# A fused attention and mixing kernel: another order of its one list of steps, with the DMA transposes of batch 3 at other places

## The chip, the cores and the metric

The kernel runs on one core of a Trainium2 chip. The metric is device time in microseconds (us) of one execution; the number given for a version is the median of its runs. The times of a profile are those of one profiled execution, counted from the first instruction of the program.

The core has five engines that each work through an instruction list of their own, in order: TensorE (PE, matmuls; its weight loads are listed as PEld), VectorE (DVE), ScalarE (ACT), GpSimd (POOL) and SyncE (SP). SP does no arithmetic here; it issues DMAs. An engine that waits for a semaphore holds back all that stands behind it in its list. Matmuls write to PSUM, which has eight banks.

## The reference

Four batches of 768 tokens. An attention with 8 heads of 64 and a local window, and then a token and channel mixing of its output:

```python
scores = scale * np.matmul(q, k.transpose(0, 1, 3, 2))
scores = scores + bias[None, :, :, :]          # -slope(head) * distance
scores = np.where(keep, scores, -1000000000.0) # 96 nearest earlier keys and the first 8
...
a = a / (np.sum(a, axis=-1, keepdims=True) + 1e-09)
return np.matmul(a, v).astype(np.float32)
```

```python
theta = x @ w_theta
cos_t, sin_t = (np.cos(theta), np.sin(theta))
zr = x * cos_t
zi = x * sin_t
yr = np.einsum('ts,bsd->btd', w_tok_r, zr)
yi = np.einsum('ts,bsd->btd', w_tok_i, zi)
y = yr + yi
u = x + y
return (u + np.maximum(u @ w_ch, 0.0)).astype(np.float32)
```

Here x is the attention's output with its heads side by side (768 x 512 per batch).

## The kernel before

The whole work is cut into 660 steps. A list of words, `order`, holds them in one sequence; a loop at the end reads a word such as `pd.3.2.1` and calls the step `pd` with the arguments 3, 2, 1. Scheduling is by hand for all five engines: each engine gets its instructions in the order in which the list names them, and only semaphores (for data, for a reused buffer, for a reused PSUM bank) hold an engine back. A second list of digits says which PSUM bank each step takes. So the list sets the order on each engine, and not the time: a step of SP that stands behind a step of GpSimd in the list does not wait for it.

The first argument of a step is the batch (0 to 3), for most. In the attention the second is a pair of heads (0 to 3); T is 128, so a batch has six token tiles.

- Loads, issued by GpSimd: `lq` (q and k of some heads), `lv` (v), `lw`, `lt`, `lc` (the three weights). Batch 3 is loaded by `lq.3.0.4` (heads 0 to 3) and `lq.3.4.4` (heads 4 to 7), each as eight DMAs of one head, and `lv.3.0.8`. Between the first and the second stands `gt.1.2`, a copy of one element on GpSimd which waits until `z.1.1.0` has written its part; so the second half and v of batch 3 are issued only then.
- qT and kT (64 x 2 heads on partitions): for batches 0 to 2, `pc` copies a pair of q (last argument 0) or k (1) together on DVE, `q` transposes it on PE, and `qe` copies the result out of PSUM. For batch 3, `pd` is one DMA transpose issued by SP (L312), 128 x 768 in two bytes, so 192 KB. `kg` (L322, L323) copies keys shifted by a tile next to the 8 global keys (kG), on DVE or ACT; it needs kT.
- `s` (L362): scores of two token tiles; `e` (L374): exponential on ACT; `x` (L383, L386): times a table of biases on DVE, which `bt` has made. `vg` (L397, L398) prepares v as `kg` does k; `v` (L421): weights times v; `n` (L432, L434): division by the sum, into x_sb.
- xT: `xd` (L443) is a DMA transpose of a pair of heads of x_sb, issued by SP; for some pairs `xt` on PE and `xe` do it. `th` (L477): theta, in parts (`th.b.c.0` and `.6` use the pairs 0 to 2 of xT, `.3` the pair 3); `sn` (L487, L489): sine and cosine on ACT (`sin` loads their table ahead); `z` (L498): zr and zi on DVE.
- `w` and `we`: transposes of the two token weights and their copies out. `m` (L511): four matmuls of the token mixing of one token tile; `u` (L519): x + y on DVE.
- uT: `ud` (L529) is a DMA transpose of a tile of u (128 KB) issued by SP, or `ut` on PE with the copy `ue` (L539). `c` (L550): four matmuls with w_ch, which need uT; `r` (L558): the sum with the relu on DVE; `st` (L564): the store of 256 KB, issued by SP, the last half by ACT.

A letter at the end of a copy step (`.a`, `.v`) says on which of ACT and DVE it is made. qT, kT and kG have six buffers each, u six, uT five, o four, x_sb two, xT one.

SP's list in the stretch in question, before:

```
xd.1.0 st.0.1 xd.1.1 st.0.0 pd.3.1.0 st.0.2 ud.1.0 ud.1.1 pd.3.0.0 pd.3.2.1 ud.1.2 pd.3.1.1 st.0.3
xd.2.0 st.0.5 xd.2.2 xd.2.1 pd.3.0.1 st.0.4 pd.3.3.1 st.1.0 ud.1.4 ud.1.5 ud.1.3 pd.3.2.0 st.1.1 pd.3.3.0
```

Of the kernel before, what the change touches and what calls it, by code (L numbers as in the profile page):

```python
# [16 lines left out]
def kernel(  # L17
# [105 lines left out]
    dist = const.tile([T, 6, T], BF)  # L123
# [20 lines left out]
    diag = const.tile([T, H, T], BF)  # L144
# [422 lines left out]
    def do(op, *a):  # L567
        ops[op](*a)
# [1 line left out]


    order = """
        warm.1.3 diag.2 warm.6.0 dist diag.0 bt.6 diag.1 sb.0.1 cast.1.1.a cast.0.0.v warm.3.1 bt.0
        cast.0.1.a diag.3 cast.1.0.v bt.4 q.0.1.0 q.0.0.0 qe.0.1.0.v.2 q.0.0.1 qe.0.0.0.a.0
        qe.0.0.1.a.0 qe.0.0.0.a.1 q.0.1.1 kg.0.0.0.1.v qe.0.0.1.v.1 lw.0 sb.0.0 qe.0.1.1.a.2 swap
        s.0.0.0 kg.0.0.1.4.a sb.0.2 kg.0.1.0.4.v q.0.2.0 lt.0.2 e.0.0.0 q.0.2.1 qe.0.2.0.v.2 lt.2.4
        s.0.0.1 s.0.0.2 e.0.0.1 sb.1.0 qe.0.2.1.v.2 s.0.1.0 warm.1.2 e.0.1.0 sb.1.1 kg.0.2.0.4.v
        sb.1.2 vg.0.0.4 e.0.0.2 s.0.1.1 lw.2 s.0.1.2 sb.2.0 e.0.1.2 v.0.0.0.0.6 v.0.0.1.0.6 e.0.1.1
        s.0.2.0 n.0.0.1.0.6 lq.1.0.8 q.0.3.0 e.0.2.0 q.0.3.1 n.0.0.0.0.6 sb.2.1 qe.0.3.1.a.2
        qe.0.3.0.v.2 s.0.2.1 v.0.1.0.0.6 e.0.2.1 xt.0.0.0.6 sb.3.1 xe.0.0.0.6.v sb.3.0 kg.0.3.0.4.v  # L580
        sb.2.2 mv.1 s.0.2.2 s.0.3.1 n.0.1.0.0.6 e.0.2.2 s.0.3.0 v.0.1.1.0.6 vg.0.4.4 e.0.3.0 sb.3.2
# [68 lines left out]
_INS = ['q', 'k', 'v', 'n_global', 'n_local', 'moe_w_theta', 'moe_w_tok_r', 'moe_w_tok_i', 'moe_w_ch']  # L650
_OUTS = [((4, 768, 512), 'float32')]
# [30 lines left out]
```

## Time and profile before

| what | value |
|---|---|
| median of 3 runs | 169.82 us (169.81 to 170.51) |
| the profiled execution | 170.19 us |
| its span, first to last instruction | 168.1 us |
| granted TensorE clock | 1.00 |
| busy: PE / DVE / ACT / POOL | 154.2 / 124.8 / 106.6 / 38.5 us |
| instructions | 3796 |

How to read the lines: in a group, `x24 | 16.2, 684 | 11.2 <-PE bank L511 11.0` means 24 instructions that were busy for 16.2 us in total, of 684 ns each, and 11.2 us in which the engine stood idle just before them, 11.0 of them ended by a PE instruction of line 511. A timeline line starts with the time of its first instruction and the time that the group took; in brackets stands the idle time before it and what ended it. A line of the chain has start, duration and what it was; "DMA kT<-qk" there is the time from the issue of that transpose to its landing. SP's and POOL's DMA lines give the time of the issue, not of the transfer. PE's matmuls overlap each other, so a group's busy time is not a sum of durations.

### The profile page before, as it was taken

What the parts mean: (1) busy time and instruction counts of PE and PEld (TensorE: products, weight loads), DVE (VectorE), ACT (ScalarE), POOL (GpSimd) and SP (SyncE); (2) the same over time, 40 slices, a digit from 0 to 9 for tenths busy, and PEclk for the clock granted to TensorE, in tenths of its full rate; (3) what the DMA queues carried; (4) which work ended last, traced back from release to release, by engine and by line L of the source; (5) the groups of instructions that cost most, each with busy time, mean ns of one, the idle gap of its engine ahead of it and who ended that gap; (6) DMA issues with size and microseconds to landing.
All of it is one profiled execution on the core that took longest, in us unless ns stands there. A gap on an engine that the chain in (4) does not pass through costs nothing.

```text
span 168.1 us, 3796 instructions
## 1 busy us (share of the span) xinstructions
PE 154.2 (92%) x1547; PEld 86.2 (51%) x1569; DVE 124.8 (74%) x257; ACT 106.6 (63%) x142; POOL 38.5 (23%) x46
## 2 busy tenths in 40 slices
PE   7899999999999996999987798899999999999990
PEld 2456685555657573545553543345557444444450
DVE  7697986978999998695994991588789438543571
ACT  3899899898789937898866115988871349100010
POOL 8975348050352102079400000000000000000000
PEclk9999999999999999999999999999999999999999
DMA  5999999999999999989999998560125674344456
GB/s 150 199 171 177 209 209 203 204 208 188 149 199 193 148 191 149 78 137 121 154 118 146 205 108 207 113 156 4 31 47 158 127 172 174 100 44 125 125 206 231
DMA packets 72704, 25.34 MB, mean 151 GB/s; under 512 B 60784, under 2 KB 69744, under 8 KB 72688
## 3 DMA queue, kind: packets, MB, share of 16 engines
q0 software_dynamic: 45696, 12.45, 82.0%
q1 hardware_dynamic: 26576, 12.13, 34.8%
q10 hardware_dynamic: 416, 0.52, 0.9%
q8 instruction: 12, 0.20, 0.5%
q14 instruction: 4, 0.03, 0.1%
HBM read 25.69 MB, written 6.29 MB: 190 GB/s over the span
## 4 chain that ended last, share of the span: by engine, by line
PE 59%; DMA 18%; DVE 15%; issue 2%; SPq 2%; ACT 1%; POOL 0%; DVEq 0%; POOLq 0%
PE bank L511 27%; PE bank L477 9%; PE bank L550 9%; DMA kT<-qk 8%; DMA xT<-x_sb 6%; PE bank L362 4%; PE bank L421 4%; DMA qk<-in_q_dram 3%; DVE e L383 2%; DVE x_sb L434 2%; DVE kT L299 2%; PE bank L265 2%; SPq L312 1%; DMA uT<-u 1%; DVE kG L322 1%
## 5 line engine op out<-in xcount | busy, mean ns | idle before, releaser
L511 PE MATMUL bank<-zri,w_tokT 128*128 128x512 bf16 x273 | 66.8, 379 | 1.4 <-issue 1.0
L374 ACT ACTIVATE e<-bank 128x1024 bf16<-128x1024 f32 (+1 forms) x48 | 42.9, 955 | 8.9 <-PE bank L362 8.3
L511 PEld LDWEIGHTS <-w_tokT 128*128 128x128 bf16 x288 | 26.5, 98 | 29.5 <-DVE w_tokT L269 0.2
L550 PE MATMUL bank<-w_ch_bf,uT 128*128 128x512 bf16 (+1 forms) x98 | 24.1, 370 | 2.4 <-DVE u L519 1.6
L477 PE MATMUL bank<-w_theta_bf,xT 128*128 128x512 bf16 x92 | 22.8, 379 | 2.9 <-DMA xT<-x_sb 2.7
L519 DVE TENSOR_TENSOR u<-x_sb,bank 128x512 bf16<-128x512 bf16 x24 | 16.2, 684 | 11.2 <-PE bank L511 11.0
L558 DVE SCALAR_TENSOR_TENSOR o<-bank,u 128x512 f32<-128x512 f32 (+1 forms) x25 | 16.2, 666 | 7.9 <-PE bank L550 7.5
L498 DVE TENSOR_TENSOR zri<-x_sb,cs 128x1024 bf16<-128x1024 bf16 (+1 forms) x30 | 16.6, 580 | 6.1 <-ACT cs L489 4.0
L434 DVE TENSOR_TENSOR x_sb<-bank,rec 128x768 bf16<-128x768 f32 (+2 forms) x21 | 16.1, 767 | 0.7
L550 PEld LDWEIGHTS <-uT 128*128 128x128 bf16 x100 | 9.3, 98 | 12.3 <-issue 1.8
L477 PEld LDWEIGHTS <-xT 128*128 128x128 bf16 x96 | 8.8, 97 | 13.0 <-DMA xT<-x_sb 3.9
L539 ACT COPY uT<-bank 128x512 bf16<-128x512 bf16 x5 | 2.9, 589 | 19.1 <-PE bank L535 19.1
L383 DVE TENSOR_TENSOR e<-e,etab 128x1024 bf16<-128x1024 bf16 (+1 forms) x24 | 14.1, 618 | 0.9 <-ACT e L374 0.9
L421 PEld LDWEIGHTS <-e 128*128 128x128 bf16 x352 | 12.6, 97 | 3.3 <-issue 1.0
L362 PE MATMUL bank<-qT,kT 64*128 64x128 bf16 x224 | 12.9, 218 | 0.4 <-DVE qT L299 0.3
L421 PE MATMUL bank<-vn,e 128*128 128x65 bf16 x224 | 13.2, 193 | 0.1
L489 ACT ACTIVATE cs<-bank,halfpi 128x1024 bf16<-128x1024 f32 x8 | 8.9, 1116 | 6.2 <-PE bank L477 6.2
L362 PEld LDWEIGHTS <-kT 64*128 64x128 bf16 x224 | 8.6, 94 | 6.3 <-issue 5.4
L92 POOL DMA_DIRECT2D vn<-in_v_dram x5 | 9.6, 1922 | 8.1 <-DVE qkn L306 6.9
L362 PE MATMUL bank<-qT,kG 64*128 64x128 bf16 x128 | 10.7, 216 | 0.0
L421 PE MATMUL bank<-vG,e 128*128 128x65 bf16 x128 | 10.4, 193 | 0.1
L86 POOL DMA_DIRECT2D qk<-in_q_dram x8 | 6.9, 864 | 12.4 <-issue 4.7
(76 smaller groups left out, 199.1 us busy)
## 6 DMA issues: line engine op xcount, KB each, us to landing
out_dram<-o SPq DMA_DIRECT2D x23, 256.0 KB, 2.4
vn<-in_v_dram POOLq DMA_DIRECT2D x3, 768.0 KB, 23.1
qk<-in_q_dram POOLq DMA_DIRECT2D x2, 768.0 KB, 20.3
qk<-in_k_dram POOLq DMA_DIRECT2D x2, 768.0 KB, 22.3
w_nat<-in_moe_w_tok_r_dram POOLq DMA_DIRECT2D x3, 384.0 KB, 12.3
w_nat<-in_moe_w_tok_i_dram POOLq DMA_DIRECT2D x3, 384.0 KB, 13.5
vn<-in_v_dram POOLq DMA_DIRECT2D x2, 384.0 KB, 9.8
qk<-in_q_dram POOLq DMA_DIRECT2D x8, 96.0 KB, 9.5
```

Of the source, the lines that this page charges most:

```text
L92: nc.gpsimd.dma_start(out=vn[:, h0:h0 + n, :, 0:D].rearrange("p h t d -> p (h t) d"), in_=v[b, h0:h0 + n].rearrange("h (t p) d -> p (h t) ...
L362: nc.tensor.matmul(pb[:, hh, o:o + T], lhsT=lhsT, rhs=qT[R, (own, nxt)[part]], start=bool(b), stop=bool(b) or (jt == NT - 1 or (j == 1 and ...
L374: nc.scalar.activation(e_c, ps_of["s", b, p, c][:, :, 0:blocks(c) * T], AF.Exp, scale=scale)
L383: nc.vector.tensor_mul(e_c, e_c, tab[:, :, s0:s0 + n].rearrange("p a s n -> p a (s n)"))
L421: nc.tensor.matmul(po4[:, head - h0, it - i0], lhsT=l_, rhs=r_, start=(i_ == 0), stop=(i_ == len(mms) - 1))
L434: nc.vector.tensor_mul(xv, po4[:, :, :, 0:D], rec.to_broadcast([T, m_, nt, D]))
L477: nc.tensor.matmul(ps_of["th", b, c][j_], lhsT=xT_sb[b][:, dc, (2 * c + j_) * T:(2 * c + j_ + 1) * T], rhs=w_theta_bf[:, dc, :], start=(dc ...
L498: nc.vector.tensor_mul(zri[b][:, i_, tt, :].rearrange("p j (g d) -> p j g d", g=NP), x_sb[b][:, :, tt, :].rearrange("p g j d -> p j g d"), ...
L511: nc.tensor.matmul(ps_of["m", b, tt], lhsT=w_tokT[wi][:, st, tt * T:(tt + 1) * T], rhs=zri[b][:, wi, st, :], start=(mixed[b, tt] == 0), st ...
L519: nc.vector.tensor_add(u_sb[b, tt].rearrange("p (g d) -> p g d", g=NP), x_sb[b][:, :, tt, :], ps_of["m", b, tt].rearrange("p (g d) -> p g ...
L550: nc.tensor.matmul(ps, lhsT=uTs[b, tt][:, dc, :], rhs=w_ch_bf[:, dc, own], start=(dc == 0), stop=(dc == NC - 1))
L558: nc.vector.scalar_tensor_tensor(o_sbs[b, tt][:, own], in0=ps_of["c", b, tt, part], scalar=0.0, in1=u_sb[b, tt][:, own], op0=ALU.max, op1= ...
```

## The change

The list is replaced by another order of the same steps, and the bank digits with it. No step is added or left out; 34 copy steps change between ACT and DVE, 17 in each direction. GpSimd's sequence of steps stays as it is. SP's list in the same stretch is now:

```
xd.1.0 xd.1.1 st.0.0 st.0.1 pd.3.0.1 pd.3.1.1 ud.1.0 st.0.5 xd.2.0 st.0.4 ud.1.3 pd.3.3.1 xd.2.1
xd.2.2 st.0.2 pd.3.0.0 ud.1.2 st.0.3 ud.1.5 ud.1.1 pd.3.1.0 pd.3.2.1 st.1.3 pd.3.3.0 pd.3.2.0 ud.1.4
```

In the common list `lv.3.0.8` stands behind `pd.3.1.0`, `ud.1.0` and `ud.1.1` before, and behind `pd.3.0.1`, `pd.3.1.1` and `ud.1.0` now. The diff, cut to the rows of interest (the last rows of both parts are the end of the list):

```diff
...
-        s.0.0.1 s.0.0.2 e.0.0.1 sb.1.0 qe.0.2.1.v.2 s.0.1.0 warm.1.2 e.0.1.0 sb.1.1 kg.0.2.0.4.v
-        sb.1.2 vg.0.0.4 e.0.0.2 s.0.1.1 lw.2 s.0.1.2 sb.2.0 e.0.1.2 v.0.0.0.0.6 v.0.0.1.0.6 e.0.1.1
...
-        x.1.2.1 xd.1.0 s.1.3.0 ue.0.3.a n.1.1.2.0.6 m.0.4.2 we.5.1.a st.0.1.2 m.0.5.0 e.1.3.0
-        x.1.2.0 xd.1.1 pc.2.0.0 s.1.2.2 u.0.4 s.1.3.1 e.1.2.2 s.1.3.2 st.0.0.2 m.0.5.2 pc.2.0.1
...
-        z.1.0.0 ut.0.5 q.2.2.1 sn.1.1.0 th.1.2.6 z.1.0.1 m.1.0.0 vg.2.0.8 pd.3.1.0 sin.1 sn.1.1.1
-        th.1.2.3 m.1.1.0 z.1.1.0 st.0.2.2 sn.1.2.0 z.1.1.1 c.0.4.2 gt.1.2 sn.1.2.1 z.1.2.0 lq.3.4.4
-        m.1.1.1 r.0.4.2 qe.2.2.1.a.2 m.1.0.1 z.1.2.1 ue.0.5.v s.2.0.2 s.2.0.0 s.2.0.1 m.1.0.2
-        e.2.0.0 m.1.1.2 e.2.0.1 u.1.0 c.0.5.2 ud.1.0 e.2.0.2 u.1.1 s.2.1.1 r.0.5.2 s.2.1.0 ud.1.1
-        s.2.1.2 e.2.1.0 x.2.0.1 m.1.2.0 lv.3.0.8 pc.2.3.1 pd.3.0.0 x.2.0.0 e.2.1.1 m.1.3.0 x.2.0.2
-        q.2.2.0 x.2.1.1 pd.3.2.1 q.2.3.1 qe.2.2.0.a.2 m.1.2.1 qe.2.3.1.v.2 kg.2.2.0.4.a q.2.3.0
-        m.1.2.2 e.2.1.2 qe.2.3.0.v.2 s.2.2.0 u.1.2 s.2.2.2 s.2.2.1 e.2.2.0 x.2.1.2 m.1.3.2 ud.1.2
-        e.2.2.1 x.2.2.0 v.2.0.2.0.6 pd.3.1.1 kg.2.3.0.4.v m.1.5.0 e.2.2.2 n.2.0.2.0.6 m.1.3.1
-        st.0.3.2 x.2.1.0 xd.2.0 s.2.3.2 x.2.2.1 s.2.3.0 s.2.3.1 e.2.3.0 m.1.5.1 kg.3.2.0.4.v
-        st.0.5.2 u.1.3 e.2.3.2 m.1.5.2 x.2.2.2 e.2.3.1 x.2.3.2 c.1.1.2 x.2.3.0 kg.3.1.0.4.a
-        v.2.2.2.0.6 x.2.3.1 v.2.1.2.0.6 n.2.2.2.0.6 m.1.4.0 n.2.1.2.0.6 xd.2.2 v.2.3.2.0.6 c.1.0.2
-        n.2.3.2.0.6 xd.2.1 m.1.4.1 r.1.1.2 m.1.4.2 pd.3.0.1 r.1.0.2 xt.2.3.0.6 u.1.4 th.2.0.0
-        st.0.4.2 xe.2.3.0.6.a u.1.5 pd.3.3.1 th.2.1.0 kg.3.0.0.4.a th.2.0.6 st.1.0.2 th.2.1.6 ud.1.4
-        kg.3.3.0.4.v th.2.0.3 th.2.2.0 sn.2.0.0 ud.1.5 th.2.1.3 th.2.2.6 sn.2.0.1 ud.1.3 c.1.2.2
-        sin.2 sn.2.1.0 z.2.0.1 c.1.5.2 pd.3.2.0 z.2.0.0 sin.3 sn.2.1.1 th.2.2.3 r.1.2.2 m.2.0.0
-        st.1.1.2 z.2.1.0 sn.2.2.0 pd.3.3.0 z.2.1.1 m.2.1.0 r.1.5.2 sn.2.2.1 c.1.3.2 z.2.2.0 m.2.0.1
...
-        c.3.5.1 r.3.4.2 st.3.3.2 c.3.5.0 r.3.5.1 st.3.4.2 r.3.5.0 st.3.5.1 st.3.5.0
...
...
+        kg.0.2.0.4.v e.0.1.0 s.0.1.1 lw.2 vg.0.0.4 s.0.1.2 sb.2.0 e.0.1.2 v.0.0.1.0.6 v.0.0.0.0.6
...
+        xt.0.0.0.6 xe.0.1.0.6.a n.0.2.1.0.6 warm.1.2 v.0.3.2.2.4 v.0.3.2.4.6 we.0.0.a n.0.3.2.2.4
...
+        m.0.0.1 bt.3 we.3.0.v m.0.0.2 we.2.1.a qe.1.0.0.v.2 we.2.0.a m.0.1.2 pc.1.0.1 pc.1.1.0 bt.2
...
+        kg.1.0.0.4.v qe.1.3.1.a.2 qe.1.3.0.v.2 w.5.0 w.5.1 we.5.0.a ut.0.1 m.0.2.2 ue.0.1.v we.3.1.a
+        we.5.1.v s.1.0.1 pc.1.2.1 ue.0.0.a s.1.0.0 kg.1.1.0.4.v lq.3.0.4 w.4.1 e.1.0.0 u.0.2 c.0.0.2
...
+        ut.0.3 m.0.4.1 ue.0.3.v xd.1.0 x.1.1.1 s.1.2.0 r.0.1.2 s.1.3.0 e.1.2.0 s.1.2.1 x.1.1.2
...
+        s.1.3.1 ue.0.2.v s.1.3.2 xd.1.1 s.1.2.2 e.1.3.1 x.1.3.0 m.0.5.0 x.1.2.1 e.1.3.2 st.0.0.2
...
+        qe.2.1.0.a.2 m.0.5.1 r.0.4.2 v.1.3.2.0.6 sin.1 xt.1.2.0.6 n.1.3.2.0.6 q.2.1.1 xe.1.2.0.6.a
...
+        th.1.1.0 xe.1.3.0.6.a r.0.3.2 th.1.0.6 kg.2.0.0.4.a pc.2.3.1 q.2.2.1 th.1.0.3 qe.2.2.1.v.2
+        th.1.1.6 sn.1.0.0 th.1.2.0 sn.1.0.1 th.1.1.3 z.1.0.0 th.1.2.6 sn.1.1.0 z.1.0.1 ut.0.5
+        pd.3.0.1 th.1.2.3 ue.0.5.v m.1.1.0 sn.1.1.1 z.1.1.0 m.1.0.0 sn.1.2.0 gt.1.2 z.1.1.1 m.1.1.1
+        lq.3.4.4 r.0.2.2 sn.1.2.1 z.1.2.0 pd.3.1.1 m.1.0.1 z.1.2.1 s.2.0.2 s.2.0.0 s.2.0.1 vg.2.0.8
+        m.1.0.2 e.2.0.0 m.1.1.2 u.1.0 e.2.0.2 c.0.5.2 ud.1.0 e.2.0.1 u.1.1 q.2.3.1 kg.2.2.0.4.a
+        r.0.5.2 s.2.1.2 s.2.1.0 qe.2.3.1.v.2 s.2.1.1 st.0.5.2 e.2.1.0 m.1.2.0 lv.3.0.8 x.2.0.2
+        e.2.1.1 m.1.3.0 x.2.0.1 x.2.1.0 e.2.1.2 q.2.3.0 q.2.2.0 m.1.2.1 qe.2.3.0.a.2 qe.2.2.0.v.2
+        m.1.2.2 x.2.0.0 kg.2.3.0.4.v s.2.2.0 s.2.2.1 x.2.1.2 e.2.2.0 s.2.2.2 x.2.1.1 m.1.3.1 u.1.2
+        e.2.2.2 v.2.0.2.0.6 e.2.2.1 x.2.2.2 m.1.5.0 n.2.0.2.0.6 m.1.3.2 x.2.2.0 xd.2.0 s.2.3.0
+        s.2.3.1 u.1.3 e.2.3.0 s.2.3.2 m.1.5.1 kg.3.0.0.4.v st.0.4.2 x.2.2.1 e.2.3.2 ud.1.3
+        v.2.1.2.0.6 kg.3.1.0.4.a m.1.4.0 n.2.1.2.0.6 pd.3.3.1 e.2.3.1 v.2.2.2.0.6 x.2.3.2 m.1.5.2
+        xd.2.1 n.2.2.2.0.6 m.1.4.1 x.2.3.1 xd.2.2 c.1.3.2 x.2.3.0 m.1.4.2 u.1.5 st.0.2.2 pd.3.0.0
+        v.2.3.2.0.6 u.1.4 c.1.0.2 n.2.3.2.0.6 ud.1.2 th.2.0.0 xt.2.3.0.6 st.0.3.2 th.2.0.6 ud.1.5
+        xe.2.3.0.6.v th.2.1.0 vg.3.0.8 th.2.0.3 ud.1.1 th.2.2.0 sn.2.0.0 r.1.3.2 th.2.1.6 pd.3.1.0
+        r.1.0.2 sn.2.0.1 th.2.2.6 th.2.1.3 pd.3.2.1 z.2.0.1 c.1.5.2 sn.2.1.0 z.2.0.0 th.2.2.3
+        st.1.3.2 r.1.5.2 sin.3 sin.2 c.1.1.2 pd.3.3.0 sn.2.2.0 z.2.1.0 c.1.2.2 r.1.1.2 sn.2.1.1
+        pd.3.2.0 kg.3.2.0.4.v m.2.0.0 r.1.2.2 sn.2.2.1 ud.1.4 m.2.1.0 kg.3.3.0.4.v z.2.1.1 s.3.1.0
...
+        st.3.1.2 c.3.5.1 st.3.2.2 r.3.4.2 c.3.5.0 st.3.4.2 r.3.5.0 r.3.5.1 st.3.5.0 st.3.5.1
...
```

## The prediction

> **What bounds the kernel now.** I read the page first, then the busy time by stage, then the idle gaps of TensorE (PE) in order of time, and last the chain and the DMA landings behind each gap.
>
> ```profile
> span 168.1 us, 3796 instructions
> PE 154.2 (92%) x1547; PEld 86.2 (51%) x1569; DVE 124.8 (74%) x257; ACT 106.6 (63%) x142; POOL 38.5 (23%) x46
> DMA  5999999999999999989999998560125674344456
> ```
>
> PE is busy for 154.2 of 168.1 us, and the change adds or removes no matmul. So it can only win or lose the other 13.9 us. The DMA row is full until slice 23 (about 96 us): loads are running all that time. The busy time by stage (us, then busy time of PE, PEld, DVE, ACT, POOL, clock, DMA, GB/s) says where the 13.9 lie:
>
> ```profile
> 12.00:62.00 50.00, 49.26 (x665) 32.45 (x669) 44.03 (x105) 43.05 (x58) 17.53 (x18) 1.00 1.72 190
> 62.00:112.00 50.00, 43.68 (x380) 23.09 (x386) 37.38 (x68) 35.30 (x49) 10.29 (x11) 1.00 1.47 145
> 112.00:160.00 48.00, 47.42 (x365) 23.67 (x371) 30.55 (x50) 18.88 (x22) 0.00 (x0) 1.00 0.40 98
> ```
>
> Of the idle time 6.3 us lie in 62-112, only 0.7 in 12-62 and 0.6 in 112-160; the rest is start and tail. The timeline of PE in that middle stage, and its groups, name the waits:
>
> ```profile
> 65.30 1.67 PE L477 MATMUL bank<-w_theta_bf,xT 128*128 128x512 bf16 x7 [1.57 <-DMA xT<-x_sb]
> ...
> 93.22 1.02 PE L550 MATMUL bank<-w_ch_bf,uT 128*128 128x512 bf16 x4 [1.56 <-DVE u L519]
> ...
> 101.59 4.71 PE L477 MATMUL bank<-w_theta_bf,xT 128*128 128x512 bf16 x20 [1.13 <-DMA xT<-x_sb]
> ```
>
> ```profile
> L550 PE MATMUL bank<-w_ch_bf,uT 128*128 128x512 bf16 x35 | 9.2, 379 | 2.4 <-DVE u L519 1.6 <-DMA uT<-u 0.7
> ```
>
> The chain (start, us, what) shows that these are DMA transposes which take long to land. The second wait, "DVE u", is one too: on VectorE (DVE), `u.1.3` stands behind `kg.3.2`, and that waits for a kT transpose.
>
> ```profile
> 55.59 9.44 DMA xT<-x_sb
> ...
> 81.91 10.14 DMA kT<-qk
> 92.07 0.30 DVE kG L322
> ...
> 102.12 2.76 DMA kT<-qk
> ```
>
> The landings of L312's transposes (qT and kT) in 50-112 give the two states: 2.7 us at best, 10.1 at worst.
>
> ```profile
> DMA to landing us min/median/max: 2.7/2.8/10.1
> ```
>
> One by one: transposes issued while GpSimd's loads of batch 3 run took 5.0 (`ud.1.0`), 5.2, 6.3, 10.1 (`pd.3.2.1`), 8.5 (`ud.1.2`), 8.3 and 7.2 us; those issued from 100 on, after the v load landed (issued 79.44, 15.7 us to landing, so 95.1), took 2.4 or 2.8.
>
> **What is moved.** All 660 steps are the same but for 34 copies that change between DVE and ScalarE (ACT): 17 each way, so the totals stay. Issued before within the loads of heads 4-7 and v: `ud.1.0`, `ud.1.1`, `pd.3.0.0`, `pd.3.2.1`, `ud.1.2`, `pd.3.1.1`, `xd.2.0`. The new SyncE (SP) list has `pd.3.0.1` and `pd.3.1.1` first (their data is complete at 70.7, when DMA is quiet), then only `ud.1.0` before the v load; behind it come `xd.2.0`, `ud.1.3`, `pd.3.3.1`, `xd.2.1`, `xd.2.2`, `pd.3.0.0`, `ud.1.2`, `ud.1.5`, `ud.1.1` and the last four `pd`. Nothing makes SP wait for the load: what holds `xd.2.0` back is `n.2.0`. GpSimd's order is the same, and its gate still opens after `z.1.1.0`.
>
> **The sum**, against the profiled execution's 170.19 us (span 168.1 and 2.1 around it; the median of the runs, 169.82, is 0.37 less). To place steps I laid each engine's new list end to end with the rows' durations (four matmuls 0.86 us, an s step 0.18-0.23, v 0.67, six transposes 0.34).
>
> 1. *xT of batch 1* (-1.57). `xd.1.0` is issued about 2.5 us sooner, the store between it and `xd.1.1` goes behind both, and PE has 1.1 us more work in front of `th.1.0.0`. The landings were 61.0, 61.7 (store) and 65.0; I put the last at 61-63.3 and PE's arrival at 64. If the transpose itself is as late as before, the 1.1 us of cover still hide most. Bounds -0.5 to -1.57.
> 2. *The copy beside the v load's issue* (-0.62). `pc.2.3.1` took 1.88 us where its fifteen likes took 0.35, while GpSimd issued the v load; PE waited 0.35 for it, and 0.27 for the next copy:
>
> ```profile
> 80.03 1.88 DVE L306 COPY qkn<-qk 128x768 bf16<-128x768 bf16 x1
> ```
>
> ```profile
> 79.44 2.28 POOL L92 DMA_DIRECT2D vn<-in_v_dram  x1
> ```
>
> It now stands before `th.1.0.3`, some 10 us ahead of that issue. What meets GpSimd's issues instead is `vg.2`; `vg.1` met such issues at 49.7 and took 1.60 against `vg.3`'s 1.43: 0.17 on DVE, hidden. Bounds -0.35 to -0.62. [...]
> 3. *kG in front of u* (-1.56). The first kG copy on DVE is now `kg.3.0`, behind `u.1.3`; its `pd.3.0.1` was issued 15 us before. `kg.3.2` and `kg.3.3` come after `r.1.1.2`, about 102 us. SP issues one transpose per 1.24 us; from `xd.2.2` at 91.3 on, `pd.3.2.1` is reached at 100 and lands at 102.6: just in time. Behind `kg.3.2` on DVE wait `z.2.1.1` and with it `m.2.0.1`, 1.1 us later. Bounds 0 to -1.56.
> 4. *xT and uT of batch 2* (-1.13 and -0.74). `xd.2.2` is issued at 91.3; with 2.8 us it lands at 94.1, and PE reaches `th.2.0.0` at 94.5. `ud.1.5` lands near 99, `c.1.5.2` comes at 99.6. Bounds 0 to -1.87.
> 5. *A wait that comes back* (+0.5). `c.1.3.2` is reached at 91.2 and needs `ud.1.3`, issued at 87.2: 89.6 if the load is over, 95.7 with the 8.5 us of `ud.1.2`. All later work of PE stands behind it. The gate opens about 1 us sooner than at 72.4. The loads behind it took 22 us beside seven transposes and a store. The v load of batch 2 beside two transposes and two stores took 10.3 from landing to landing (55.6 to 65.9), the one of batch 1 alone 6.2 (41.6 to 47.8): so about 1 us for each. With two of them the loads end near 88-89. Bounds 0 to +4.5.
> 6. *Start* (+0.5). `v.0.0.1` is reached at 13.4 and vG is ready at 14.3; 0.3 of the 0.9 come back, as a warm-up matmul that filled this place is done later. Bounds 0 to +0.9.
> 7. *ACT and DVE* (+0.4). Before `e.1.0.0` ACT has 3.4 us more work (among it `we.2.0`, `we.2.1`, `we.3.1`, `we.5.0` and bias tables that were done earlier); PE has 2.5 us more there, and ACT's idle time in 31-41 was 1.7: hidden, at most +0.9. The Sin table load (1.28 us) now falls where ACT idled 2.63 at 62. From 73 on banks are handed over with under 0.2 us to spare (`c.0.5.2` behind `e.2.0.0`, `s.2.1.1` behind `e.2.0.1`): 0.4, up to 1.0.
> 8. *Tail* (+0.2). `r.3.5.1` now follows `r.3.5.0`, and the last store is ACT's: 0 to +0.42, one half-width `r`.
>
> Removed 5.62, added 1.6: -4.0. From 170.19 that is 166.2, on the median **165.8 us**. With every wait of the middle stage gone and nothing added it is 169.82 - 6.3 = 163.5.
>
> [...]
>
> **Rivals.** (a) *The waits only move.* SP's place behind the v load's issue is not behind its landing. If `xd.2.0`, `ud.1.3` and `xd.2.1` still share the engines with it, `ud.1.3` lands near 95.7, PE waits 3-4.5 at `c.1.3.2`, and terms 3 to 5 are eaten; terms 1 and 2 less 6 to 8 remain: about 169.3. For it: only `n.2.0` and `u.1.3` separate them from the load. Against: DMA's load was half transposes in that stretch, and these are gone. That the change does not do what it says ends here too.
>
> (b) *Slower: the gate opens late.* `gt.1.2` waits for DVE's `z.1.1.0`, so for ACT's Sin row. If the heavier ACT brings that from 72.4 to 76 or later, the loads end at 93 or later, and the transposes, now bunched behind them, all land in them: `ud.1.3` near 97, `xd.2.2` near 101, PE 6-7 us behind the above. It decides from `z.1.1.0` at about 75.5, where the 4 us are gone; at 77 the time is 171.5. Against: ACT idled 6.4 us over its waits in 35-68, more than its 3.4 of new work.
>
> **How the numbers follow.** Forecast 0.60 (163.5 to 168.0); (a) 0.24 (168.0 to 170.6), half of it within 0.5%, about 0.85 us and what a measurement of this kernel can tell from no change; (b) 0.16. So faster 0.72, same 0.12, slower 0.16; the range reaches from 163.5 through (a), to 170.6.
>
> **What would show it.** Right: PE's idle time in the stretch that was 62-112 down to about 2 us; no wait of PE on xT near 64; `pc.2.3.1` at 0.35; `kg.3.0` on DVE without a wait; the v load landing before 90; L312's worst landing under 5. Wrong: a wait of PE L550 on uT above 2 us before 100 (a); the gate after 75 (b); DVE waiting for kT in front of L498 (term 3); PE idle above 2 us in 12-62 (terms 6, 7).

## The result, and the profile after

| version | median, us | against the kernel before (95% interval) | span of the profiled run, us |
|---|---|---|---|
| before | 170.06 (20 runs beside the changed kernel) | 1 | 168.1 |
| changed | 169.24 (20 runs, 168.17 to 170.16) | 0.9957 [0.9938, 0.9976] | 167.1 |

The change makes the kernel 0.4% faster, 0.8 us. That is within the 0.5% that the prediction called the limit of what can be told from no change, and a fifth of the forecast 4.0 us. The ratios, here and below, leave out runs that took over 1.5% longer than the fastest of the same kernel; the medians don't. The page's first lines, busy time of each engine and the DMA row:

```profile
span 167.1 us, 3827 instructions
...
PE 156.7 (94%) x1569; PEld 86.5 (52%) x1569; DVE 124.6 (75%) x256; ACT 107.0 (64%) x143; POOL 39.1 (23%) x46
...
DMA  5999999999999999979999985973007760515556
```

PE's busy time seems to have grown by 2.5 us. The matmuls are the same: the trace of before lacks 22 of the 1569 matmul records, as the x1547 in its line shows. So the waits are read one by one, not as differences of busy time, and the 13.9 us of idle time that the prediction starts from are too many, by about those 2.5. The windows (the columns are those of before):

```profile
12.00:62.00 50.00, 49.40 (x662) 31.95 (x657) 43.37 (x101) 46.25 (x62) 18.07 (x18) 1.00 1.72 187
62.00:112.00 50.00, 47.44 (x441) 25.19 (x440) 39.72 (x74) 36.48 (x50) 10.36 (x11) 1.00 1.30 146
112.00:160.00 48.00, 46.45 (x345) 22.60 (x344) 27.99 (x47) 15.71 (x19) 0.00 (x0) 1.00 0.40 101
```

The middle stage is as the prediction wanted it: 2.6 us of PE idle where there were 6.3. But 112 to 160, where it looked for nothing, now has 1.55 us idle where there were 0.6. The timeline of PE, groups with a named wait of 0.2 us or more after 60:

```profile
65.52 1.90 PE L477 MATMUL bank<-w_theta_bf,xT 128*128 128x512 bf16 x8 [0.20 <-DMA xT<-x_sb]
...
98.42 0.39 PE L477 MATMUL bank<-w_theta_bf,xT 128*128 128x512 bf16 x1 [1.66 <-DMA xT<-x_sb]
...
109.05 0.21 PE L362 MATMUL bank<-qT,kT 64*128 64x128 bf16 x1 [0.68 <-DVE o L558]
...
131.72 2.98 PE L477 MATMUL bank<-w_theta_bf,xT 128*128 128x512 bf16 x13 [0.47 <-DMA xT<-x_sb]
...
134.97 0.61 PE L477 MATMUL bank<-w_theta_bf,xT 128*128 128x512 bf16 x2 [0.27 <-DMA xT<-x_sb]
...
149.12 2.75 PE L511 MATMUL bank<-zri,w_tokT 128*128 128x512 bf16 x12 [0.81 <-DVE o L558]
```

Of the six waits of before that made the forecast's 5.62 us, four are gone: nothing waits near 81 to 93, where 0.35, 0.27 and 1.56 stood, nor for a uT, where 0.74 stood. The first, 1.57, is down to 0.20 at 65.52. The sixth, for xT in front of `th.2.0.0`, is not gone: it was 1.13 and is 1.66. L550's group on the page, which had 2.4 us of idle time in before's middle stage, has none in the whole program:

```profile
L550 PE MATMUL bank<-w_ch_bf,uT 128*128 128x512 bf16 (+1 forms) x100 | 23.8, 370 | 0.0
```

With that one five waits stand behind 96, 3.89 us. Up to 96 the forecast came about: of its waits 3.75 us lay there, and 0.20 is left. Behind 96 more than half of it is given back: 3.89 us of waits where there were 1.87. The chain of waits says to whom (start, us, what; DMA and SPq pieces of 60 to 152):

```profile
94.19 4.18 DMA xT<-x_sb
105.78 2.43 DMA out_dram<-o
...
132.17 2.75 DMA xT<-x_sb
...
145.03 3.22 DMA out_dram<-o
```

Two of the four are not transposes but stores. A store is on the chain because o has four buffers: a step `r` on DVE waits until the store four `r` steps ago has landed, and with it wait the PSUM bank that it should empty and PE, which needs the bank. The DVE timeline shows one of these waits, and a kT transpose that came late, in a row:

```profile
107.27 0.29 DVE L322 COPY kG<-kT 128x512 bf16<-128x512 bf16 x1 [1.13 <-DMA kT<-qk]
...
108.30 0.69 DVE L558 SCALAR_TENSOR_TENSOR o<-bank,u 128x512 f32<-128x512 f32 x1 [0.53 <-DMA out_dram<-o]
```

All of these are issued by SP. SP's timeline (start, time that the issue took):

```profile
87.33 1.21 SPq L443 DMA_TRANSPOSE xT<-x_sb  x1
88.60 1.47 SPq L564 DMA_DIRECT2D out_dram<-o  x1
90.16 1.20 SPq L529 DMA_TRANSPOSE uT<-u  x1
91.55 1.21 SPq L312 DMA_TRANSPOSE kT<-qk  x1
92.85 2.58 SPq L443 DMA_TRANSPOSE xT<-x_sb  x2
95.48 1.59 SPq L564 DMA_DIRECT2D out_dram<-o  x1
97.17 1.24 SPq L312 DMA_TRANSPOSE qT<-qk  x1
98.47 1.26 SPq L529 DMA_TRANSPOSE uT<-u  x1
99.78 0.57 SPq L564 DMA_DIRECT2D out_dram<-o  x1
100.44 2.53 SPq L529 DMA_TRANSPOSE uT<-u  x2
103.08 1.23 SPq L312 DMA_TRANSPOSE qT<-qk  x1
104.48 1.21 SPq L312 DMA_TRANSPOSE kT<-qk  x1
105.78 0.53 SPq L564 DMA_DIRECT2D out_dram<-o  x1
```

SP issues from 87.33 on without a break; a transpose takes it 1.2 us, a store 0.5 to 1.6. The second half of the group at 92.85 is `xd.2.2`, issued at 94.19 though `n.2.2` had ended at 92.74. `pd.3.2.1` goes out at 104.48, and `st.1.3` at 105.78, its data ready since 101.7. Ahead of 87.33 SP stood idle for 8 us behind `xd.2.0`, which waited for `n.2.0`.

### The profile page after: what moved, and what is told of

Read it like the earlier page. It is cut to its first block, busy times and chain, and to the rows that moved or that the text cites. A ratio compares the mean times of both kernels' runs of the same rounds, so it can differ in the third digit from the quotient of the medians.

```text
span 167.1 us, 3827 instructions
## 1 busy us (share of the span) xinstructions
PE 156.7 (94%) x1569; PEld 86.5 (52%) x1569; DVE 124.6 (75%) x256; ACT 107.0 (64%) x143; POOL 39.1 (23%) x46
## 4 chain that ended last, share of the span: by engine, by line
PE 62%; DMA 13%; DVE 13%; issue 5%; ACT 4%; SPq 2%; DVEq 0%
PE bank L511 26%; DMA xT<-x_sb 9%; PE bank L477 8%; PE bank L550 6%; PE bank L362 5%; PE bank L421 4%; DMA out_dram<-o 3%; PE bank L237 3%; PE bank L265 3%; DVE o L558 2%; PE bank L294 2%; DVE x_sb L434 2%; DVE u L519 2%; PE bank L291 2%; DVE zri L498 1%
## 5 line engine op out<-in xcount | busy, mean ns | idle before, releaser
L511 PE MATMUL bank<-zri,w_tokT 128*128 128x512 bf16 x288 | 69.2, 379 | 0.8 <-DVE o L558 0.8
L511 PEld LDWEIGHTS <-w_tokT 128*128 128x128 bf16 x288 | 26.3, 98 | 29.8 <-issue 1.9
L477 PE MATMUL bank<-w_theta_bf,xT 128*128 128x512 bf16 x96 | 23.4, 379 | 2.6 <-DMA xT<-x_sb 2.6
L498 DVE TENSOR_TENSOR zri<-x_sb,cs 128x1024 bf16<-128x1024 bf16 (+1 forms) x30 | 16.3, 581 | 10.5 <-ACT cs L489 8.6
L550 PE MATMUL bank<-w_ch_bf,uT 128*128 128x512 bf16 (+1 forms) x100 | 23.8, 370 | 0.0
L550 PEld LDWEIGHTS <-uT 128*128 128x128 bf16 x100 | 9.4, 98 | 9.8 <-DMA uT<-u 0.2
L86 POOL DMA_DIRECT2D qk<-in_k_dram x8 | 7.2, 906 | 6.5 <-DMA vn<-in_v_dram 6.5
```

The lines of the kernel that those rows point to most:

```text
L86: nc.gpsimd.dma_start(out=pair.rearrange("p (t h d) -> p t h d", t=NT, h=2)[:, :, h % 2], in_=(q, k)[i_][b, h].rearrange("(t p) d -> p t d ...
L477: nc.tensor.matmul(ps_of["th", b, c][j_], lhsT=xT_sb[b][:, dc, (2 * c + j_) * T:(2 * c + j_ + 1) * T], rhs=w_theta_bf[:, dc, :], start=(dc ...
L498: nc.vector.tensor_mul(zri[b][:, i_, tt, :].rearrange("p j (g d) -> p j g d", g=NP), x_sb[b][:, :, tt, :].rearrange("p g j d -> p j g d"), ...
L511: nc.tensor.matmul(ps_of["m", b, tt], lhsT=w_tokT[wi][:, st, tt * T:(tt + 1) * T], rhs=zri[b][:, wi, st, :], start=(mixed[b, tt] == 0), st ...
L550: nc.tensor.matmul(ps, lhsT=uTs[b, tt][:, dc, :], rhs=w_ch_bf[:, dc, own], start=(dc == 0), stop=(dc == NC - 1))
```

## The experiments

Theory G, after this reading: the gain was there at 96, and SP's new list gave it back at four places. Rival R: the engines behind (ACT's sines, DVE) set the pace, and a wait taken away comes back at the next step. Four runs moved SP's steps at one place each; nothing else differs from the changed kernel. The times are given against the kernel before, so they stand beside the changed kernel's 0.9957; 0.0059 is 1 us.

**The xT of batch 2 sooner.** SP, from `xd.2.0` on:

```diff
-xd.2.0 st.0.4 ud.1.3 pd.3.3.1 xd.2.1 xd.2.2 st.0.2 pd.3.0.0 ud.1.2 st.0.3 ud.1.5
+xd.2.0 ud.1.3 xd.2.1 xd.2.2 pd.3.3.1 st.0.4 st.0.2 pd.3.0.0 ud.1.2 st.0.3 ud.1.5
```

> The changed kernel with two steps moved on SP only: pd.3.3.1 and st.0.4 now stand behind xd.2.2 and not in front of it. Theory G (the forecast's gain was there and SP's new queue gave it back): xd.2.2 is issued at 92.8 instead of 94.2, the last xT of batch 2 lands at 95.6 to 97.0 instead of 98.4, and PE's wait of 1.66 us in front of th.2.0.0 shrinks to between 0 and 0.3; the time goes down by 0.6 to 1.6 us, to 167.6-168.6. Rival R (the engines behind, above all ACT's sines and DVE's z, set the pace, and a wait taken away comes back at the next step): th.2.0.0 starts earlier, but PE waits as much more in front of m.2.0.0 or s.3.0.2; the time moves by less than 0.3.

Measured: 169.84 us, ratio 0.9999 [0.9967, 1.0031]: no gain over the changed kernel, whose interval overlaps this one. `xd.2.2` was issued at 92.9 and landed at 95.66, and the wait before `th.2.0.0` is gone. PE's timeline has this instead:

```profile
103.67 1.04 PE L550 MATMUL bank<-w_ch_bf,uT 128*128 128x512 bf16 x4 [2.12 <-DMA uT<-u]
```

This is `c.1.5.2`, and its `ud.1.5` was issued at 101.2, with its data ready since 94.7. So theory G's time was wrong and rival R's, no gain, was right, but R's reason was not: the wait went not to an engine but to the next step of SP's list. From here comes theory Q: SP's issuing itself is the bound between 87 and 112.

**The store and the kT transpose sooner.**

```diff
-pd.3.1.0 pd.3.2.1 st.1.3 pd.3.3.0
+st.1.3 pd.3.2.1 pd.3.1.0 pd.3.3.0
```

> The changed kernel with two steps moved on SP only: st.1.3 (the store that frees one of o's four buffers) and then pd.3.2.1 (the transpose kg.3.2 needs) stand in front of pd.3.1.0. Theory G: st.1.3 is issued some 2.5 us sooner, pd.3.2.1 as early as before or 0.1 later; DVE's wait of 0.53 for the buffer in r.1.2.2 is gone, that of 1.13 for kT stays or shrinks, and PE's waits at m.2.0.1, m.2.0.2 and s.3.0.2 (together 1.1) shrink to 0.5 or less; the time goes down by 0.5 to 1.1 us. Rival R: DVE reaches z.2.1.1 no sooner, or PE waits for the next of DVE's results; less than 0.3.

Measured: 168.95 us, 0.9943 [0.9915, 0.9971], 0.2 us below the changed kernel, which the intervals can't tell from nothing. In its trace the wait of 0.68 before `s.3.0.2` is gone, DVE's 1.13 and 0.53 with it, and the waits for xT near 131 and 134 stand at 0.63 and 0.24. The place is right; its price remains unclear.

**The xT of batch 3 sooner.**

```diff
-ud.2.3 xd.3.0 xd.3.1 xd.3.2 ud.2.2 st.2.0 xd.3.3 ud.2.1
+xd.3.0 xd.3.1 xd.3.2 ud.2.2 st.2.0 xd.3.3 ud.2.3 ud.2.1
```

> The changed kernel with three steps moved on SP only: xd.3.0 in front of u.2.3 and so of ud.2.3; ud.2.2 behind xd.3.2; ud.2.3 behind xd.3.3. Theory G: xd.3.0 is issued at about 123 instead of 125.4, and the last xT that th.3.1.0 needs lands at 129.5-130.5 instead of 131.7; PE's waits of 0.47 and 0.27 near 131.7 and 135.0 go, and the time goes down by 0.7 to 1.1 us. Rival R: xd.3.2 and xd.3.3 hang on v and n and are issued as late as now, or c.2.2 and c.2.3 now wait for the uT that was put back; less than 0.3, or a little slower.

Measured: 168.29 us, 0.9905 [0.9867, 0.9943]: 0.9 us below the changed kernel, with intervals that just touch. `xd.3.0` was issued at 121.1 and `xd.3.2` landed at 130.24; both waits for xT are gone, and 0.19 for a uT came. Theory G.

**The last stores of batch 1 sooner.** `st.1.4` and `st.1.1` go from their places near 145 and 135 to right behind `r.1.4`:

```diff
-ud.2.0 ud.2.3 xd.3.0 ... ud.2.1 st.1.1 ud.2.4 st.2.3 ud.2.5 st.2.2 st.1.4 st.2.1
+ud.2.0 st.1.4 st.1.1 ud.2.3 xd.3.0 ... ud.2.1 ud.2.4 st.2.3 ud.2.5 st.2.2 st.2.1
```

> The changed kernel with two stores moved on SP only: st.1.4 right behind r.1.4 and st.1.1 behind it, some 25 us sooner. Theory G: r.2.4 finds its o buffer free, DVE's idle 4.9 us in front of it are gone, r.2.1 behind it comes sooner and frees its bank, and PE's wait of 0.81 in front of m.3.2.0 near 149 goes; the time goes down by 0.8 to 1.0 us. Rival R: the bank that m.3.2.0 waits for comes free as late as now, since r.2.1 waits for something else; less than 0.3.

Measured: 168.27 us, 0.9912 [0.9884, 0.9941], 0.8 us below, again with intervals that just touch. `st.1.4` was issued at 117.62 and no longer at 145.03, and no wait before `m.3.2.0` is left. Theory G.

**SP's list lighter and in the order of need.** The next run takes three stores out of the crowded stretch and puts the rest in the order in which it is waited for:

```diff
-pd.3.0.1 pd.3.1.1 ud.1.0 st.0.5
-xd.2.0 st.0.4 ud.1.3 pd.3.3.1 xd.2.1 xd.2.2 st.0.2 pd.3.0.0 ud.1.2 st.0.3 ud.1.5 ud.1.1
-pd.3.1.0 pd.3.2.1 st.1.3 pd.3.3.0
+st.0.4 st.0.3 pd.3.0.1 pd.3.1.1 st.0.2 ud.1.0 st.0.5
+xd.2.0 ud.1.3 xd.2.1 xd.2.2 ud.1.5 pd.3.0.0 ud.1.2 ud.1.1
+pd.3.2.1 pd.3.1.0 st.1.3 pd.3.3.1 pd.3.3.0
```

> The changed kernel with SP's list alone made lighter between 87 and 112, where the run with the two steps behind xd.2.2 showed SP issuing without a break and the wait coming back at c.1.5.2 for uT: st.0.4 and st.0.3 go in front of pd.3.0.1 and st.0.2 in front of ud.1.0, where SP stood idle (together 3.6 us of SP's time); behind xd.2.2 come ud.1.5, pd.3.0.0, ud.1.2, ud.1.1, pd.3.2.1, pd.3.1.0, st.1.3, pd.3.3.1. Theory Q (SP's issue rate, 1.2 to 1.3 us for a transpose, bounds 87 to 112, so that moving single steps in the list only moves the wait, and less work for SP removes it): xd.2.2 is issued at 92.8-93.5, ud.1.5 lands by 99.5, pd.3.2.1 by 104; the waits of 1.66 before th.2.0.0 and of 0.68 before s.3.0.2 go and none above 0.3 takes their place up to 110; the time falls by 1.8 to 2.9 us below the changed kernel's. Rival R (ACT and DVE set the pace up to 110): PE idles as much, in front of other steps; less than 0.6 us.

Measured: 167.01 us, 0.982 [0.9779, 0.9862], 2.3 us below the changed kernel. `xd.2.1`, `xd.2.2` and `ud.1.5` were each issued within 0.03 us of their data. The longest wait of PE that is left between 90 and 112 is this:

```profile
107.40 0.21 PE L362 MATMUL bank<-qT,kT 64*128 64x128 bf16 x1 [0.31 <-DVE o L558]
```

**Each half alone.** The three stores sooner, with the transposes in the order of the changed kernel:

```diff
-pd.3.0.1 pd.3.1.1 ud.1.0 st.0.5 xd.2.0 st.0.4 ud.1.3 pd.3.3.1 xd.2.1 xd.2.2 st.0.2 pd.3.0.0 ud.1.2 st.0.3 ud.1.5
+st.0.4 st.0.3 pd.3.0.1 pd.3.1.1 st.0.2 ud.1.0 st.0.5 xd.2.0 ud.1.3 pd.3.3.1 xd.2.1 xd.2.2 pd.3.0.0 ud.1.2 ud.1.5
```

> The changed kernel with nothing moved but three stores of batch 0, whose data is ready at 63, 67 and 74: st.0.4 and st.0.3 in front of pd.3.0.1, st.0.2 in front of ud.1.0. The order of the transposes stays that of the changed kernel. Theory Q (it is the number of SP's instructions behind 87 that counts, not their order): nearly the gain of the lighter list, 1.6 to 2.4 us below the changed kernel, with xd.2.2 issued by 93.2 and pd.3.2.1 by 101.5. Rival O (the order of the transposes made the gain, as ud.1.5 and xd.2.2 came sooner): 0 to 0.8 us.

Measured: 168.05 us, 0.9899 [0.9867, 0.9932], 1.0 us. `pd.3.3.1` still stood in front of `xd.2.2`, which was issued at 93.95 and landed at 98.17, so the wait before `th.2.0.0` was left:

```profile
98.22 0.39 PE L477 MATMUL bank<-w_theta_bf,xT 128*128 128x512 bf16 x1 [1.31 <-DMA xT<-x_sb]
```

And the order of need alone, with the three stores behind `ud.1.5` and `ud.1.2`:

```diff
-xd.2.0 st.0.4 ud.1.3 pd.3.3.1 xd.2.1 xd.2.2 st.0.2 pd.3.0.0 ud.1.2 st.0.3 ud.1.5 ud.1.1
-pd.3.1.0 pd.3.2.1 st.1.3 pd.3.3.0
+xd.2.0 ud.1.3 xd.2.1 xd.2.2 ud.1.5 st.0.4 st.0.2 pd.3.0.0 ud.1.2 st.0.3 ud.1.1
+pd.3.2.1 pd.3.1.0 st.1.3 pd.3.3.1 pd.3.3.0
```

> The other half of the lighter list: the changed kernel with SP's steps behind 87 in the better order (xd.2.1, xd.2.2, ud.1.5, then st.0.4, st.0.2, pd.3.0.0, ud.1.2, st.0.3, ud.1.1, pd.3.2.1, pd.3.1.0, st.1.3, pd.3.3.1), but with the three stores still behind 87. The stores alone gave 1.0 us, both together 2.3. Theory O (each step must go out in the order in which it is waited for, and with that three stores more cost nothing): 1.6 to 2.4 us below the changed kernel, ud.1.5 issued by 95.5, no wait of PE above 0.5 up to 110. If the two halves simply add up: 1.0 to 1.5, with a wait of 0.3 to 1.0 near 103 to 107 where the three stores push ud.1.1 and pd.3.2.1 back. Theory Q in its strict form (the number of instructions alone): 0 to 0.6.

Measured: 169.34 us, 0.9962 [0.9934, 0.9989]: nothing. `ud.1.5` was issued at 95.03 and PE had no wait between 66 and 103, but `st.0.3` landed only at 103.59, and DVE's `r.1.0`, which needs its buffer, stood behind it, and behind that PE's `c.1.1.2`, and 0.78 more before its next group (DVE's timeline, then PE's):

```profile
103.61 0.69 DVE L558 SCALAR_TENSOR_TENSOR o<-bank,u 128x512 f32<-128x512 f32 x1 [3.30 <-DMA out_dram<-o]
```

```profile
104.36 1.02 PE L550 MATMUL bank<-w_ch_bf,uT 128*128 128x512 bf16 x4 [1.18 <-DVE o L558]
```

The order alone did what theory Q in its strict form said, but the stores alone did less than it said. The halves, 1.0 and 0, do not add up to 2.3. With this many steps behind 87, each of the orders tried leaves one of xT, uT and o's buffers late; with three fewer, one order serves all. An order that leaves the three stores behind 87 with `st.0.3` further ahead was not tried.

**Transposes put back beside the v load.** Does it matter at all that they were moved out? First in the changed kernel:

```diff
-ud.1.0 st.0.5 xd.2.0
+ud.1.0 st.0.5 ud.1.1 pd.3.0.0 pd.3.2.1 xd.2.0
```

> The changed kernel with three transposes put back beside the v load: ud.1.1, pd.3.0.0 and pd.3.2.1 are issued right behind st.0.5, at about 79 to 83, and no longer at 97 to 106. Theory L (the load makes them land late and they make the load land late, and this cost the kernel before its time): they take 5 to 10 us to land, the v load lands at 92 to 94 instead of 90.6, xd.2.0 and ud.1.3 take 4 to 8 us, PE waits 1 us or more at c.1.3.2 and 3 us or more before th.2.0.0; slower by 1 to 3 us. Theory Q (what counts in the changed kernel is SP's crowded list behind 87, and nobody waits for these three): they land just as late, but 3.8 us of SP's time leave the stretch behind 97; the wait before th.2.0.0 stays within 0.5 of 1.66, that before s.3.0.2 goes; the time falls by 0.3 to 1.2 us.

Measured: 171.09 us, 1.8 above the changed kernel by the medians; but the ratio, 0.9964 [0.9908, 1.0019], rests on four of its twelve runs and shows no loss. The last section says what divides its runs. So the time decides nothing, and the trace is read for its landings. The three took 5.7, 7.5 and 8.2 us instead of 2.4, 2.9 and 2.8, the v load landed at 94.56 instead of 90.61, `xd.2.0` took 7.7 instead of 4.0 and `ud.1.3` 6.7 instead of 2.5:

```profile
96.28 1.89 PE L550 MATMUL bank<-w_ch_bf,uT 128*128 128x512 bf16 x4 [2.83 <-DMA uT<-u]
```

That is the wait at `c.1.3.2` of theory L. To have its price without the rest, two of them were put back in the kernel with the lighter list:

```diff
-st.0.5 xd.2.0 ud.1.3 xd.2.1 xd.2.2 ud.1.5 pd.3.0.0 ud.1.2 ud.1.1 pd.3.2.1
+st.0.5 pd.3.0.0 pd.3.2.1 xd.2.0 ud.1.3 xd.2.1 xd.2.2 ud.1.5 ud.1.2 ud.1.1
```

> The kernel with the lighter SP list, and two transposes put back beside the v load: pd.3.0.0 and pd.3.2.1 right behind st.0.5, at 79.5 to 82, instead of 97 to 101. SP is not crowded here, so this prices the transposes beside the load alone. Theory L: they land 6 to 9 us after their issue, the v load lands 1 to 2.5 us later, ud.1.3 lands at 94 to 95.5 instead of 92.75, so that PE waits 0.5 to 2 us at c.1.3.2; 0.5 to 2 us above the run with the lighter list (167.0). Rival (nobody is hurt, as all their readers come late): within 0.4 us of it.

Measured: 167.61 us, 0.9879 [0.9824, 0.9934], 0.6 us above the lighter list by the medians and 1.0 by the ratios, whose intervals overlap. They took 5.1 and 9.3 us to land, the v load landed at 93.28 instead of 91.34, and:

```profile
94.48 1.04 PE L550 MATMUL bank<-w_ch_bf,uT 128*128 128x512 bf16 x4 [1.16 <-DMA uT<-u]
```

For the landings theory L holds in these runs: the transposes put beside the load were late themselves (5.1 to 9.3 us) and made the load late, by 4.0 and 1.9 us, and in the first run the next transposes, by 3.7 and 4.2. What this costs in time is not settled.

**Two terms of the sum alone, in the kernel before.** Its kG copy `kg.3.2` behind `r.1.1` on DVE, and nothing else:

```diff
-kg.3.2.0.4.v st.0.5.2 u.1.3 ... r.1.1.2
+st.0.5.2 u.1.3 ... r.1.1.2 kg.3.2.0.4.v
```

> The kernel before with one step moved on DVE alone: kg.3.2 behind r.1.1 instead of in front of u.1.3; SP's list and all transposes stay as they were. The forecast's third term by itself: PE's wait of 1.56 before L550 near 93, for u.1.3, goes; if nothing comes back the time falls by 1.2 to 1.6 us from 170. Rival (the wait only moves): PE arrives sooner at th.2.0.0 and waits 2.0 to 2.7 for xT there instead of 1.13, since xd.2.0 lands at 96.9 and xd.2.1 at 101.5 because of the load and SP; the time falls by less than 0.5.

Measured: 168.62 us, 0.9922 [0.9887, 0.9957], 1.3 us faster than before. The wait of 1.56 is gone, and a little of it comes back at `th.2.0.0`, 1.52 instead of 1.13:

```profile
100.34 4.71 PE L477 MATMUL bank<-w_theta_bf,xT 128*128 128x512 bf16 x20 [1.52 <-DMA xT<-x_sb]
```

By the ratios this one move of one copy gives 1.3 us and the whole change 0.7, with intervals that overlap. Then the copy `pc.2.3.1` some 12 us sooner:

```diff
-pc.2.2.1 ... lv.3.0.8 pc.2.3.1
+pc.2.2.1 pc.2.3.1 ... lv.3.0.8
```

> The kernel before with one DVE copy moved: pc.2.3.1 right behind pc.2.2.1, near 68, some 12 us ahead of GpSimd's issue of the v load. The forecast's second term by itself: the copy takes 0.35 instead of 1.88, PE's waits of 0.35 and 0.27 near 82 to 85 go; if that stays to the end the time falls by 0.35 to 0.62 us. Rival (the wait before L550 near 93, for kT and then u.1.3, ends when that transpose lands, whatever came earlier): PE waits as much more there; within 0.2 us.

Measured: 170.44 us, 1.0015 [0.9977, 1.0052]: nothing. The copy took 0.35 and its two waits are gone, and the wait for `u.1.3`, which stands behind the kT transpose that lands at 92.48, grew from 1.56 to 2.38:

```profile
93.65 1.04 PE L550 MATMUL bank<-w_ch_bf,uT 128*128 128x512 bf16 x4 [2.38 <-DVE u L519]
```

Behind this longer wait the clock of the profiled execution fell too, to 0.50 for 3.41 us (last section), so its time is not the price of the copy alone.

**All that helped, together:** the lighter list, the xT of batch 3 and the two stores sooner.

> The lighter SP list and, with it, the two moves that were run alone: the xT of batch 3 sooner (xd.3.0 before u.2.3, ud.2.2 behind xd.3.2, ud.2.3 behind xd.3.3) and st.1.4 and st.1.1 right behind r.1.4. If the three are independent, as SP's queue would have it: 1.8-2.9 + about 0.9 + about 0.8 below the changed kernel's 169.2, so 164.7 to 165.8, near what the forecast gave the change itself. If ACT or DVE stand behind (rival R): not below 167.3, what the two moves alone give.

Measured: 165.54 us (164.91 to 165.91), 0.9735 [0.9694, 0.9777]: faster than both kernels, 3.8 us below the changed one. The three alone gave 2.3, 0.9 and 0.8, together 4.0: within the intervals they add up. Its windows and the one wait of PE over 0.2 us behind 62:

```profile
62.00:112.00 50.00, 48.78 (x463) 26.35 (x470) 41.14 (x75) 37.09 (x51) 10.37 (x11) 1.00 1.42 158
```

```profile
65.53 1.90 PE L477 MATMUL bank<-w_theta_bf,xT 128*128 128x512 bf16 x8 [0.45 <-DMA xT<-x_sb]
```

Nothing but SP's list differs from the changed kernel. So the gain that the sum counted was to be had from this order of the other engines; only SP's list kept it back.

## Why the prediction was wrong

The step that failed is the walk along SP's list, in terms 3 and 4: its dates came 2.9 to 4.6 us late, and no term stood for its stores. The removals were counted rightly, and most of the forecast's signs came: `pc.2.3.1` at 0.35, `kg.3.0` without a wait, the gate at 72.0, and

```profile
DMA to landing us min/median/max: 2.7/2.8/3.3
```

for L312 in 62 to 112, where the worst had been 10.1. The v load landed at 90.6, a little behind the 90 that was asked for, and one sign of being wrong came: DVE waited for kT in front of L498 (term 3). Step by step:

- *Term 1*, xT of batch 1: 1.57 became 0.20, by cover alone: `xd.1.1` was issued at 56.66, 1.1 us later than before, and landed at 65.47, not at 61 to 63.3.
- *Term 2*: right, but only because term 3 went too. Alone it gained nothing, in a run whose clock fell (0.99 in the mean). The line of the copies (min, median and max of one in ns, first and last start) has no slow one left:

```profile
L306 DVE COPY qkn<-qk x5: 344/350/435, 60.5 to 66.6; 128x768 bf16<-128x768 bf16 x5
```

- *Term 3*: the 1.56 went, and the run with that copy moved confirms it. The clause on the other end failed. `pd.3.2.1` landed at 107.24, not 102.6, so it was not "just in time": it cost DVE 1.13, and this with the store behind it the 0.68 before `s.3.0.2`. Of the 4.6 us 2.9 are SP's later start with `xd.2.2`; the steps from there took 10.3 us, where the forecast had 8.7.
- *Term 4* is the term that failed most. `xd.2.2` was to be issued at 91.3 and land in 2.8 us. Its data came at 92.74, SP was free for it at 94.19, and it took 4.18, so that it landed at 98.37 and not at 94.1: 1.4 us for the data, 1.5 for SP and 1.4 for the landing. PE came at 96.2 instead of 94.5, and still the 1.13 to be saved became a wait of 1.66, a half more than before. The uT part, 0.74, did go.
- *Term 5* did not come: `ud.1.3` landed at 92.66, just before PE reached `c.1.3.2` at 92.90. The runs with transposes put back show how near it was: 1.16 with two, 2.83 with three.
- *Terms 6 to 8* were to cost 1.1 us and cost about 0.6. From the start of `c.3.5.0`, PE's last step, 163.41 before and 162.73 after, the tail took 4.6 and then 4.4 us, so no loss there. But the named waits fell by 1.53 and `c.3.5.0` came only 0.68 sooner: the other 0.85 lies where no view names a wait, as in matmuls a little further apart (16 of L511 took 4.05 us from 109.53 on, and 3.62 from 71.05 on). They were not what ate the gain.
- *Missing*: a term for the stores. The prediction asked of no store of the middle stage when it would land. But o's four buffers make a late store a wait of DVE, twice (0.68 in part, 0.81). Missing too are the xT of batch 3 (0.47 and 0.27), whose `xd.3.0` now stood behind `ud.2.3`; nothing behind 112 was costed, since before had no wait there.

The waits that are left, 3.89 and 0.20, are 3.6 us more than the 0.5 (term 5) that the forecast had for waits; less the 0.5 that terms 6 to 8 had too much, that is the error, 3.1 by the spans and 3.2 by the medians. Rival (a) named the time, 169.3, but by luck: its own terms (1 and 2 less 6 to 8, -1.1 from 169.82) come to 168.7, and its reason did not hold. The transposes behind `xd.2.0` did not land late in the v load (`ud.1.3`, issued 0.45 us before the load's landing, took 2.50); they were issued late by SP. The forecast walked SP's list with 1.24 us for a transpose, and asked of it four dates only (`ud.1.3`, `xd.2.2`, `ud.1.5`, `pd.3.2.1`).

## What to carry to other kernels

Steps that are moved off a crowded resource land on the queue that issues them: lay that queue's whole new list end to end, stores too, with the time at which each step's data is ready and the time at which somebody waits for it, up to the end of the program. A store is not free while its buffer is one of few: with four of them one late store made PE wait 0.81 us here. Where several waits share one issuing engine, undoing one alone may gain nothing, as with the xT of batch 2 (169.84 us against 169.24); send early what has long been ready, into the stretch where that engine idles, and order the rest by need.

## What the hardware showed besides

In two of the profiled runs a pause of PE was followed by a clock at half. In the run with three transposes put back PE stood idle for 2.83 us up to 96.28, and the windows (the granted clock is the third number from the end) read:

```profile
92.00:96.00 4.00, 1.45 (x7) 0.48 (x5) 2.89 (x5) 1.28 (x1) 0.00 (x0) 0.98 1.37 174
96.00:99.00 3.00, 2.72 (x7) 1.03 (x8) 0.00 (x0) 0.00 (x0) 0.00 (x0) 0.50 1.09 262
99.00:104.00 5.00, 4.95 (x47) 2.70 (x46) 3.66 (x6) 0.11 (x1) 0.00 (x0) 0.98 0.82 143
```

Three us at half clock make an estimated 1.5 us of loss besides the wait's length (the four matmuls at 96.28 took 1.89 us, and 1.04 in the run with two put back). In the run with the copy sooner a pause of 2.38 us ended at 93.65, and the fall came behind it:

```profile
94.53:97.94 3.41, 3.41 (x48) 2.84 (x47) 3.14 (x7) 0.83 (x2) 0.00 (x0) 0.50 1.11 266
```

After a pause of 2.12 us, in the run with the xT of batch 2 sooner, the clock stayed at 1.00. Pauses of 2.38 and 2.83 us came before the fall, in the executions that were profiled; that the pause caused it is an estimate from these three pauses, and no run tried it by itself. The clock divides the runs with three transposes put back: the mean granted clock was 1.00 in two, which took 168.15 and 168.91 us, and 0.985 to 0.99 in the other ten, which took 170.3 to 173.1 (3.4 us at half clock take 0.010 off the mean over 169 us). So what that run lost against the changed kernel's 169.24 goes with the clock.

`xd.2.2` took 4.18 us in the changed kernel, with the v load landed at 90.61, and 4.22 in the run with the three stores alone (93.95 to 98.17). The page lists 12 packets, 0.20 MB in all, of a queue that it calls `instruction` (q8); the trace of the changed kernel has one of 16 KB at 95.12, which took 1.57 us. In the traces of before and of the changed kernel 51 transposes were issued after the v load of batch 3 had landed. 7 of them took 3.68 to 4.18 us to land, and all 7 had such a packet under way between issue and landing; the other 44 took 2.38 to 2.91 us, and 4 of them had. `xd.3.0` was issued at 123.76 in before, 5 us ahead of the packet at 128.80, and landed in 2.74 us; in the changed kernel it was issued at 125.35, with a packet under way since 125.26, and took 3.68. By these counts it is likely that the packets hold the transposes up; no run moved a packet, so it is not shown.
